# Attention and experts on one core: values and chunk 4's scores as one group, GpSimd scaling chunk 4, and weight pieces begun in output buffers

## The chip, the cores and the metric

The kernel runs on one core of one Trainium2 chip. The metric is device time in microseconds. A core has five engines that run side by side and wait for each other by semaphores: TensorE (PE) multiplies matrices and writes its results to PSUM, a memory of eight banks of 128 x 512 float32 values; VectorE (DVE) and ScalarE (ACT) work on PSUM and on SBUF, the large memory; GpSimd (POOL) works on SBUF; SyncE (SP) issues DMAs. Each engine's instructions stand in an order that is settled when the program is built.

## The reference

Block-causal attention over 8 batches, 8 heads, 576 positions of 64 dimensions (blocks of 64), then a two-layer expert network over all 4608 tokens, with weights given as 64-bit floats:

```python
scores = scale * np.matmul(q, k.transpose(0, 1, 3, 2))
mask = block_i >= block_j
scores = np.where(mask, scores, -1000000000.0)
scores = scores - np.max(scores, axis=-1, keepdims=True)
attn = np.exp(scores)
attn = attn / (np.sum(attn, axis=-1, keepdims=True) + 1e-09)
...
x = np.ascontiguousarray(attn_out.transpose(0, 2, 1, 3)).reshape(B * S, H * D)
h = x @ w_in
g = h * (1.0 / (1.0 + np.exp(-1.702 * h)))
return (g @ w_out).astype(np.float32)
```

## The kernel before

**Turns.** Attention goes by pairs of heads, 32 pairs; turn n (0 to 31) works on pair n, and turn 32 ends the last one. The two heads of a pair lie on partitions 0 to 63 and 64 to 127. Queries are cut into five chunks: chunk 0 has 64 of them, chunks 1 to 4 have 128 each, and chunk i sees 64(2i+1) keys: 64, 192, 320, 448, 576. A score longer than 512 columns does not fit a bank, so chunk 4's is cut into 256 and 320 columns, one bank for each head and cut: four banks.

**Experts.** The 4608 tokens are cut into 12 tiles of 384. A tile has 16 units. A unit is twelve matmuls into the bank `hp` (tag `h`, one buffer), then on ACT a tanh (L562), on DVE the product `g`, which reads `hp` (L563), on ACT the high half `gh` (L571), on GpSimd the low half `gl` (L82); and nine matmuls into the three banks `acc` for the unit before it. Float32 accuracy comes from splitting each operand into a high and a low part.

**Which work stands where.** A string gives each turn's slots (`ORDER`, L26). A number is the scores of that chunk, `3+0/2+1` those of four chunks, `V` the sums of values of the pair before (`av`, L429), `L` the transposes of the next pair's queries and keys (`prep`, L292). `B`, `C` and `a` turn weights by TensorE in the first eight turns; from turn 8 on (`early` false) DVE and 16 DMAs do that (`turn`, L382). After each slot `advance` (L592) emits units of the experts up to a quota, so attention stands between an `hp` block and an `acc` block. The order on DVE, ACT and GpSimd is not written out: the framework's scheduler settles it when it builds the program, with higher priority for `g`, `gh` and `gl`.

**One chunk's way.** Scores lie in banks. `weigh` (L340) reads them on DVE, adds the mask, keeps the maximum (L351, each followed by a short reading of the accumulator), and ACT takes the exponential and the sum (L358). `normalise` (L364) makes the reciprocal on DVE and scales the chunk, on the engine that `SCALE_ON` (L20) names: P for GpSimd, D for DVE. `turn` transposes the result on DVE (L385, L390), and behind chunk 4 issues the 16 DMAs.

**Banks.** `bank()` (L89) hands out PSUM banks in rotation: seven before the experts begin, three while turns 4 to 8 run, four from turn 9 on. The eighth, tag `w3`, belongs until then to the weights: there are 32 pieces of 128 x 512 64-bit words, and `begin` (L215) writes a piece's upper word, scaled, into `w3` by ACT; `merge` (L221) shifts it there on DVE and puts sign and lower bits together in two further instructions; `split_weights` (L239) makes the high and low parts. Output buffers (tag `osb`, three) are idle meanwhile.

Of the kernel before, what the change touches and what calls it, by code (L numbers as in the profile page):

```python
# [16 lines left out]

SCALE_ON = ("PPPPP", "PPPPP", "PPPPD")  # L20

# [4 lines left out]
ORDER = (  # L26
# [3 lines left out]
)  # L30

START = "1+0 - B 2/3 L C - V - 4 - a - - -"
# [8 lines left out]
def attention_moe_kernel(  # L41
# [123 lines left out]
    def width(i):  # L165
        return BLK * (2 * i + 1)
# [47 lines left out]

    def begin(j):  # L215

        bits[j] = ps.tile([P, 512], F32, tag="w3", name="wm")
        for w, c in parts[j]:
            nc.scalar.activation(out=bits[j][:, c], in_=f(w[..., 1]), func=AF.Copy, scale=2.0**-112)

# [71 lines left out]
    def prep(n):  # L292

        tag = "e0" if early(n) and n % 2 else "qk"
        qk[n] = d2.tile([P, 2, S], F32, tag=tag, name="qk", bufs=1)
        for x in range(2):
            nc.vector.transpose(out=qk[n][:, x], in_=raw[n][:, x].rearrange("p c d -> p (c d)"))  # L297
        raw.pop(n)
        m = follower(n)
        if m is not None:  # L300
            load(m)

    stats = {}

    def score(n, banks):

        if n not in stats:
            mx = d2.tile([P, NCH + 1, 2], F32, tag="mx", name="mx")
            sm = d2.tile([P, NCH, 2], F32, tag="sm", name="sm")
            stats[n] = (mx, sm)  # L310
        todo = []
        for chunks in banks:

            part = []
            for lo, hi in ((0, 512),) if width(chunks[0]) <= 512 else ((0, 256), (256, S)):
                ss = [bank() for _ in range(2)]
                c = 0
                for i in chunks:
                    a, z = qrange(i)
                    w = min(hi, width(i)) - lo  # L320
                    for hd in range(2):
                        r = slice(hd * D, hd * D + D)

                        mm(
                            out=ss[hd][:, c : c + w], lhsT=qk[n][r, 0, a : a + P],
                            rhs=qk[n][r, 1, lo : lo + w], start=True, stop=True,
                        )
                        part.append((i, hd, lo, lo + w, ss[hd][0 : z - a, c : c + w]))
                    c += w
            todo.append(sorted(part, key=lambda x: (chunks[::-1].index(x[0]), x[2])))  # L330
        for chunks, part in zip(banks, todo):
            e = {}
            for i, hd, lo, hi, s in part:
                e[i] = weigh(n, i, hd, lo, hi, s, e.get(i))
            for i in chunks[::-1]:
                normalise(n, i, e[i])
                if not early(n):
                    turn(n, i, e[i])
# [87 lines left out]
                in_=src[:, x : x + 2 * len(part), a : a + 2],  # L426
            )

    def av(n):  # L429

        b, h = divmod(n, HP)
        before_av(n)
        o, o0 = bank(), bank()

        todo = []
        for i in range(1, NCH):
            c = (i - 1) * P
            todo += [(o, c, P, j, pw[:, :, SLOT[i] + j]) for j in range(i)]
            todo.append((o, c + BLK, BLK, i, pw[:, 2:4, 9 + i]))
        last = len(todo) - 1  # L440
        todo.append((o0, 0, BLK, 0, pw[:, 0:2, 10]))

        for x, (bk, c, nn, j, w) in enumerate(todo):
            for hd in range(2):
                mm(
                    out=bk[hd * D : hd * D + D, c : c + nn].rearrange("d (a c) -> d a c", c=32),
                    lhsT=values(n)[:, hd, j], rhs=w[:, :, hd], start=x in (0, last + 1), stop=x >= last,
                )
        c0 = (b % 2) * S
        nc.scalar.copy(out=xr[:, h, c0 : c0 + BLK], in_=o0[:, 0:BLK])  # L450
# [5 lines left out]
    def follower(n):  # L456

        m = {0: 2, 1: 3, 2: 4, 3: None}.get(n, n + 1)
        return None if m is None or m >= NPAIR else m

    def order(n):
        return {HP: START, 2 * HP: HANDOVER}.get(n, ORDER[phase(n)]).split()

    def step(n):
# [4 lines left out]
        def item(x):  # L469
            if x == "V":  # L470
                return (lambda: av(n - 1)) if n else None
            if x == "L":
                return (lambda: prep(n + 1)) if n + 1 < NPAIR else None
            if x in ("a", "B", "C"):
# [31 lines left out]
    def chunk_time(tt):  # L506
        return 4 * unit1(tt) + tt // P * 650
# [69 lines left out]
        yield from second(prev)  # L577


    ends = np.cumsum([0.0] + [NFC * chunk_time(tt) for _, tt in TILES])  # L580

    def quota(pos):
        xs, ys = zip(*TILES_BY)
        return -1.0 if pos < xs[0] else np.interp(pos, xs, [ends[y if y >= 0 else y - 1] for y in ys])

    def heads_for(t):
        return -(-sum(TILES[t]) // S) * H
# [36 lines left out]
    for n in range(NPAIR + 1):  # L624
        items = step(n)
        for sl, fn in enumerate(items):
            if fn is not None:
                fn()
            if order(n)[sl] == "V":
# [35 lines left out]
```

## Time and profile before

| | us |
|---|---|
| median of 3 runs | 1122.7 (1121.84 to 1124.51) |
| profiled execution | 1120.49 |
| its span, first to last instruction | 1118.6 |
| PE busy | 1076.4 (96%) |
| DVE, ACT, POOL busy | 583.0, 498.6, 406.7 |
| turn 9 begins at | 218.9 |
| turn 31 begins at | 924.0 |

PE's instructions overlap in its pipeline, so their mean durations do not add up to time; what a block takes is read from the start of its first instruction to the start of the next block's. A turn from the tenth on takes about 32 or 33 us (28 where it holds five units in place of six).

### The profile page before, as it was taken

The page shows a single profiled execution, that of the slowest core. Times are in us where ns is not written, and L with a number is a line of the kernel's source. Part 1 is how long each engine was busy: PE and PEld are TensorE (multiplying, and loading weights), DVE is VectorE, ACT ScalarE, POOL GpSimd, SP SyncE. Part 2 cuts the span into 40 slices and gives each one's busy share as a digit, 9 for nine tenths or more (in the row PEclk, how much of TensorE's full clock was granted, in tenths as well). Part 3 has the DMA queues.
Part 4 walks back from the last instruction along what each step waited for, and adds up shares of the span by engine and source line. Part 5 has one row for each costly group of instructions (what it writes and reads, how often), then busy time and mean ns, then how long its engine had stood idle before and what let it go on. Part 6 is the DMA issues. An engine that isn't in the chain of part 4 may idle for free. (4 is left out here: it accounts for less than half of the span.)

```text
span 1118.6 us, 19977 instructions
## 1 busy us (share of the span) xinstructions
PE 1076.4 (96%) x6960; PEld 908.7 (81%) x6960; DVE 583.0 (52%) x1856; ACT 498.6 (45%) x1321; POOL 406.7 (36%) x509
## 2 busy tenths in 40 slices
PE   5969998999999999999999999999999999999998
PEld 3757776788888888888888888888888888899997
DVE  6776885545545555654555655645545654211210
ACT  5866776434534433534443543444434444322322
POOL 4665664333333332333333333333333233122222
PEclk9979999999999999999999999999999999999999
DMA  8734532332444432343443333344342332200000
GB/s 171 205 89 153 150 73 62 84 79 57 105 86 86 103 80 64 64 98 78 98 101 74 75 93 65 70 108 85 81 107 63 71 85 58 54 29 1 29 1 29
DMA packets 219365, 91.25 MB, mean 82 GB/s; under 512 B 197760, under 2 KB 197760, under 8 KB 219264
## 3 DMA queue, kind: packets, MB, share of 16 engines
q1 hardware_dynamic: 214528, 89.38, 34.0%
q10 hardware_dynamic: 4736, 0.59, 0.3%
q8 instruction: 55, 0.90, 0.3%
q14 instruction: 46, 0.38, 0.1%
HBM read 45.09 MB, written 9.44 MB: 49 GB/s over the span
## 5 line engine op out<-in xcount | busy, mean ns | idle before, releaser
L82 POOL TENSOR_TENSOR gl<-g,gh 128x384 fp32r<-128x384 f32 x192 | 194.7, 1014 | 551.5 <-ACT gh L571 449.1
L99 PE MATMUL hp<-xh,wih 128*128 128x384 f32 x768 | 264.7, 345 | 7.9 <-DVE g L563 6.9
L563 DVE SCALAR_TENSOR_TENSOR g<-g,hp 128x384 f32<-128x384 f32 x192 | 105.9, 552 | 319.1 <-ACT g L562 317.8
L99 PE MATMUL hp<-xh,wil 128*128 128x384 f32 x768 | 258.4, 336 | 0.1
L562 ACT ACTIVATE g<-hp 128x384 f32<-128x384 f32 x192 | 94.1, 490 | 359.8 <-PE hp L99 354.8
L99 PE MATMUL hp<-xl,wih 128*128 128x384 f32 x768 | 253.9, 338 | 0.4 <-DVE xl L82 0.4
L99 PE MATMUL acc<-woh,gh 128*128 128x512 f32 x576 | 233.9, 406 | 0.0
L99 PE MATMUL acc<-wol,gh 128*128 128x512 f32 x576 | 226.9, 394 | 0.0
L99 PEld LDWEIGHTS hp<-xh,wih 128*128 128x128 f32 x768 | 144.2, 188 | 34.1 <-DVE g L563 23.1
L99 PE MATMUL acc<-woh,gl 128*128 128x512 f32 x576 | 167.9, 393 | 0.3 <-POOL gl L82 0.3
L571 ACT CAST gh<-g 128x384 fp32r<-128x384 f32 x192 | 98.4, 513 | 156.5 <-DVE g L563 156.4
L99 PEld LDWEIGHTS hp<-xh,wil 128*128 128x128 f32 x768 | 144.3, 188 | 6.5 <-POOL wil L82 0.7
L358 ACT ACTIVATE e<-e,mx 64x64 f32<-64x64 f32 (+4 forms) x240 | 132.3, 552 | 37.6 <-DVE mx L351 37.6
L376 POOL TENSOR_TENSOR e<-e,sm 64x64 f32<-64x64 f32 (+1 forms) x192 | 113.6, 612 | 95.0 <-DVE sm L371 46.5
L99 PEld LDWEIGHTS hp<-xl,wih 128*128 128x128 f32 x768 | 143.6, 188 | 1.3 <-DVE xl L82 1.3
L99 PE MATMUL bank<-qk 64*128 64x320 f32 (+4 forms) x768 | 122.5, 428 | 14.5 <-DVE qk L297 11.1
L99 PEld LDWEIGHTS acc<-woh,gh 128*128 128x128 f32 x576 | 107.9, 187 | 34.2 <-issue 10.5
L99 PEld LDWEIGHTS acc<-woh,gl 128*128 128x128 f32 x576 | 107.8, 188 | 25.9 <-POOL gl L82 1.2
L99 PEld LDWEIGHTS acc<-wol,gh 128*128 128x128 f32 x576 | 108.3, 188 | 16.7 <-POOL wol L82 0.3
L351 DVE CUSTOM_DVE_ANT_0 e<-bank,mask 64x64 f32<-64x64 f32 (+4 forms) x240 | 89.7, 417 | 56.9 <-PE bank L99 52.8
L385 DVE STREAM_TRANSPOSE turned<-e 128x384 f32<-128x384 f32 (+1 forms) x192 | 92.3, 499 | 48.8 <-POOL e L376 48.3
L99 PEld LDWEIGHTS bank<-qk 64*128 64x128 f32 x768 | 69.6, 193 | 54.2 <-issue 25.4
(50 smaller groups left out, 956.0 us busy)
## 6 DMA issues: line engine op xcount, KB each, us to landing
turned<-turned SPq DMA_DIRECT2D x192, 80.0 KB, 2.1
turned<-turned SPq DMA_DIRECT2D x96, 112.0 KB, 2.2
raw<-in_q_dram SPq DMA_DIRECT2D x128, 72.0 KB, 2.4
out_dram<-osb SPq DMA_DIRECT2D x36, 256.0 KB, 2.2
raw<-in_k_dram SPq DMA_DIRECT2D x120, 72.0 KB, 2.6
turned<-turned SPq DMA_DIRECT2D x96, 88.0 KB, 2.1
words<-in_moe_w_in_dram SPq DMA_DIRECT2D x16, 512.0 KB, 6.3
vp<-in_v_dram SPq DMA_DIRECT2D x60, 128.0 KB, 2.4
```

The lines of the kernel that those rows point to most:

```text
L82: eng.tensor_tensor(out=out, in0=in0, in1=in1, op=ALU.subtract)
L99: return tc.keep_in_program_order(nc.tensor.matmul(**kw))
L351: nc.vector.tensor_tensor_reduce(out=e[0:m, hd, lo:hi], in0=s, in1=mk, op0=ALU.add, op1=ALU.min, scale=-0.125, scalar=3e38 if lo == 0 else ...
L358: nc.scalar.activation(out=e[0:m, hd], in_=e[0:m, hd], func=AF.Exp, scale=-1.0, bias=mx[0:m, i, hd : hd + 1], accum_out=sm[0:m, i, hd : hd ...
L376: nc.gpsimd.tensor_tensor(out=x, in0=x, in1=sc.to_broadcast([m, width(i)]), op=ALU.mult)
L385: nc.vector.transpose(out=tw[:, :, SLOT[i] : SLOT[i] + i, hd].rearrange("p b j c -> p j b c"), in_=e[:, hd, 0 : i * P],)
L562: nc.scalar.activation(out=g, in_=hp[:, 0:tt], func=AF.Tanh, scale=1.702)
L563: nc.vector.scalar_tensor_tensor(out=g, in0=g, scalar=1.0, in1=hp[:, 0:tt], op0=ALU.add, op1=ALU.mult)
L571: nc.scalar.copy(out=gh, in_=g)
```

## The change

- `SCALE_ON`: from turn 8 on chunk 4 is scaled by GpSimd, too.
- A slot `V4` takes the place of `V` and `4` from turn 9 on (turn 8 keeps `HANDOVER`). It takes a bank, runs `av` for the pair before, with the first block of values in that bank's first 64 columns, and then chunk 4's scores. These are now 512 columns for each head in a bank of its own, and the last 64 keys of both heads in one matmul of all 128 rows, in columns 64 to 191 of the bank with the first block of values.
- For that, `prep` leaves the last 64 keys out of `qk` from turn 9's keys on and transposes them into `ends`, where each head's keys have their own columns, with zeros in the other head's rows.
- `av` computes the first block of values ahead of the others, in all turns.
- `begin` writes the first 28 pieces into output buffers in SBUF, and `w3` joins the rotation of banks until these pieces are done.
- The mask grows to 576 columns.

```diff
-SCALE_ON = ("PPPPP", "PPPPP", "PPPPD")
+SCALE_ON = ("PPPPP", "PPPPP", "PPPPP")
...
-    "3+0/2+1 - - - V - - 4 - - - L -",
+    "3+0/2+1 - - - - V4 - - - L - -",
...
         if not turns["experts"]:
             tags += ["acc0", "acc1", "acc2", "h"]
-        elif turns["n"] > 2 * HP:
+        if turns["n"] > 2 * HP or conv["step"] < 4 * len(places):
             tags.append("w3")
...
-    MW = 448
+    MW = 576
...
+    ends = sp.tile([P, 2, BLK], F32, name="ends")
+    nc.gpsimd.memset(ends, 0.0)
...
-        bits[j] = ps.tile([P, 512], F32, tag="w3", name="wm")
+        if j < 2 * len(places):
+            bits[j] = d2.tile([P, WC], F32, tag="osb", name="wb", bufs=3)
+        else:
+            bits[j] = ps.tile([P, WC], F32, tag="w3", name="wb")
...
         for x in range(2):
-            nc.vector.transpose(out=qk[n][:, x], in_=raw[n][:, x].rearrange("p c d -> p (c d)"))
+            z = QC * P if x and n > 2 * HP else S
+            nc.vector.transpose(out=qk[n][:, x, 0:z], in_=raw[n][:, x, 0 : z // 32].rearrange("p c d -> p (c d)"))
+            for hd in range(2 if z < S else 0):
+                r = slice(hd * D, hd * D + D)
+                nc.vector.transpose(
+                    out=ends[r, hd], in_=raw[n][r, x, z // 32 : S // 32].rearrange("p c d -> p (c d)")
+                )
...
-    def score(n, banks):
+    def score(n, banks, shared=None):
...
-            for lo, hi in ((0, 512),) if width(chunks[0]) <= 512 else ((0, 256), (256, S)):
+            cuts = (0, 512) if width(chunks[0]) <= 512 or shared is not None else (0, 256, S)
+            for lo, hi in zip(cuts, cuts[1:]):
...
+            if shared is not None:
+                i = NCH - 1
+                mm(
+                    out=shared, lhsT=qk[n][:, 0, slice(*qrange(i))], rhs=ends.rearrange("p h k -> p (h k)"),
+                    start=True, stop=True,
+                )
+                part += [(i, hd, QC * P, S, shared[:, hd * BLK : (hd + 1) * BLK]) for hd in range(2)]
...
-    def av(n):
+    def av(n, o0=None):
...
-        o, o0 = bank(), bank()
+        o = bank()
+        if o0 is None:
+            o0 = bank()
...
+        todo.insert(0, (o0, 0, BLK, 0, pw[:, 0:2, 10]))
         last = len(todo) - 1
-        todo.append((o0, 0, BLK, 0, pw[:, 0:2, 10]))
...
+    def values_and_4(n):
+        o0 = bank()
+        av(n - 1, o0)
+        if n < NPAIR:
+            score(n, [[NCH - 1]], o0[:, BLK : 3 * BLK])
```

What that moves is shown for turn 18, by the rows of the built programs. `hp_` and `g_` with a number are one unit's, and the two programs number them differently.

PE, before, at the end of the values: `turned` and `vp` are the values' operands, `acc` begins the next unit's work.

```order
L99 MATMUL bank_5492<-turned_75,vp_73 64x128 x6
L99 MATMUL bank_5492<-turned_75,vp_73 64x64 x2
L99 MATMUL bank_5492<-turned_75,vp_73 64x128 x8
L99 MATMUL bank_5492<-turned_75,vp_73 64x64 x2
L99 MATMUL bank_5493<-turned_75,vp_73 64x64 x2
L99 MATMUL acc0_4979<-woh_1335,gh_5457 128x512
```

PE, before, two units further on, where chunk 4's scores (`qk`) stand behind `hp_5568`:

```order
L99 MATMUL hp_5568<-xl_978,wih_1123 128x384
L99 MATMUL bank_5588<-qk_5333 128x256
L99 MATMUL bank_5589<-qk_5333 128x256
L99 MATMUL bank_5592<-qk_5333 128x320
L99 MATMUL bank_5593<-qk_5333 128x320
L99 MATMUL acc0_4979<-woh_1335,gh_5553 128x512
```

PE, after, from the values on: `bank_5516` is the shared bank, and `bank_5554` and `bank_5555` are by the rotation the banks in which chunks 2 and 1 were scored, `bank_5377` and `bank_5378` below.

```order
L99 MATMUL bank_5517<-turned_77,vp_75 64x128 x8
L99 MATMUL bank_5517<-turned_77,vp_75 64x64 x2
L99 MATMUL bank_5554<-qk_5326 128x512
L99 MATMUL bank_5555<-qk_5326 128x512
L99 MATMUL bank_5516<-ends_73,qk_5326 128x128
L99 MATMUL acc0_4973<-woh_1337,gh_5481 128x512
```

The scores of chunk 4 moved ahead by two units, next to the values, and no `acc` or `hp` stands between them any more.

DVE, after, at the same place: `hp_5496` is the last unit ahead of the values.

```order
L595 SCALAR_TENSOR_TENSOR g_5509<-g_5509,hp_5496 128x384
L407 STREAM_TRANSPOSE turned_77<-e_5388 128x3x4x32 x2
L373 ISA e_5405,mx_5369<-bank_5377,mask_69 128x192
L373 ISA mx_5369 128x1
L373 ISA e_5405,mx_5369<-bank_5378,mask_69 128x192
```

The reading of chunks 2 and 1 stands behind that unit's `g` and the two transposes of chunk 3, as it did before.

DVE, before, behind the transposes of chunk 2 (`e_5415`): two units' `g` stand ahead of and within the reading of chunk 4 (`e_5596`).

```order
L385 STREAM_TRANSPOSE turned_75<-e_5415 128x2x4x32 x2
L390 STREAM_TRANSPOSE turned_75<-e_5415 64x2x2x32
L563 SCALAR_TENSOR_TENSOR g_5552<-g_5552,hp_5539 128x384
L351 ISA e_5596,mx_5374<-bank_5588,mask_69 128x256
L351 ISA mx_5374 128x1
L563 SCALAR_TENSOR_TENSOR g_5581<-g_5581,hp_5568 128x384
```

DVE, before, from the end of that reading to the next `g`:

```order
L297 STREAM_TRANSPOSE qk_5655<-raw_5336 128x576 x2
L368 TENSOR_SCALAR sm_5375<-sm_5375 128x2
L371 RECIPROCAL sm_5375<-sm_5375 128x2
L378 TENSOR_SCALAR e_5596<-e_5596,sm_5375 128x576 x2
L385 STREAM_TRANSPOSE turned_75<-e_5596 128x4x4x32 x2
L390 STREAM_TRANSPOSE turned_75<-e_5596 64x2x2x32
L563 SCALAR_TENSOR_TENSOR g_5648<-g_5648,hp_5635 128x384
```

DVE, after, behind the transposes of chunk 2 (`e_5410`):

```order
L407 STREAM_TRANSPOSE turned_77<-e_5410 128x2x4x32 x2
L412 STREAM_TRANSPOSE turned_77<-e_5410 64x2x2x32
L373 ISA e_5559,mx_5369<-bank_5554,mask_69 128x512
L373 ISA mx_5369 128x1
L373 ISA e_5559,mx_5369<-bank_5555,mask_69 128x512
```

DVE, after, from the end of that reading to the first `g` of a unit behind the values, `hp_5598`:

```order
L306 STREAM_TRANSPOSE qk_5647<-raw_5331 128x576
L390 TENSOR_SCALAR sm_5370<-sm_5370 128x2
L393 RECIPROCAL sm_5370<-sm_5370 128x2
L407 STREAM_TRANSPOSE turned_77<-e_5559 128x4x4x32 x2
L412 STREAM_TRANSPOSE turned_77<-e_5559 64x2x2x32
L595 SCALAR_TENSOR_TENSOR g_5611<-g_5611,hp_5598 128x384
```

The whole of chunk 4 now stands directly behind chunk 2, ahead of every `g` of the units behind the values; the two scalings left DVE (GpSimd has them, and the transposes wait for it), and the keys' transposes moved behind that `g`. In other turns of the changed program this `g` stands a few rows further up: between the two 512-wide transposes in turns 12, 13, 14, 17 and 25; right behind the reciprocal in 9, 19, 20, 22, 27, 28 and 30; behind three subtractions for a new tile in 16 and 24. The two transposes of chunk 3 stand ahead of the last unit's `g` in turns 9, 16, 19, 22, 24, 27 and 30, and in turn 10 the whole reading of chunks 2 and 1 does.

More of the change, by code (lines that the diff above doesn't have):

```diff
@@ L446, in av @@
                     out=bk[hd * D : hd * D + D, c : c + nn].rearrange("d (a c) -> d a c", c=32),
-                    lhsT=values(n)[:, hd, j], rhs=w[:, :, hd], start=x in (0, last + 1), stop=x >= last,
+                    lhsT=values(n)[:, hd, j], rhs=w[:, :, hd], start=x in (0, 1), stop=x in (0, last),
                 )
@@ L471, in item @@
                 return (lambda: av(n - 1)) if n else None
+            if x == "V4":
+                return lambda: values_and_4(n)
             if x == "L":
@@ L577, in moe @@
         yield from second(prev)
-    ends = np.cumsum([0.0] + [NFC * chunk_time(tt) for _, tt in TILES])
+    tile_ends = np.cumsum([0.0] + [NFC * chunk_time(tt) for _, tt in TILES])
     def quota(pos):
         xs, ys = zip(*TILES_BY)
-        return -1.0 if pos < xs[0] else np.interp(pos, xs, [ends[y if y >= 0 else y - 1] for y in ys])
+        return -1.0 if pos < xs[0] else np.interp(pos, xs, [tile_ends[y if y >= 0 else y - 1] for y in ys])
     def heads_for(t):
@@ L628, in attention_moe_kernel @@
                 fn()
-            if order(n)[sl] == "V":
+            if order(n)[sl][0] == "V":
                 heads_done = 2 * n
```

## The prediction

> **What bounds the kernel now.** I read the page first, then the windows, then PE's timeline inside one turn, because a share of 96% says that PE is the limit but not where it waits.
>
> ```profile
> span 1118.6 us, 19977 instructions
> PE 1076.4 (96%) x6960; PEld 908.7 (81%) x6960; DVE 583.0 (52%) x1856; ACT 498.6 (45%) x1321; POOL 406.7 (36%) x509
> 0.00:218.90 218.90, 186.05 (x1335) 145.16 (x1335) 155.13 (x472) 143.72 (x394) 122.47 (x152) 0.96 0.48 124
> 252.40:1118.60 866.20, 857.63 (x5413) 735.62 (x5412) 411.10 (x1327) 342.61 (x893) 273.41 (x343) 1.00 0.31 71
> PE hp L99 <- DVE g L563: 6.9, 7, 1.8
> ```
>
> The first nine turns (0 to 218.9 us) hold 32.9 us of idle PE; from the eleventh turn on PE is idle for 8.6 us in 866. So there whatever makes PE wait is added to the time whole. The last row, from PE's waits, names the only engine that can still hold the experts up: VectorE, by reading `hp`. There is one PSUM bank for `hp`, so the next unit's first matmul cannot start until DVE's `g` of the unit before is done.
>
> The middle of a settled turn on PE (the timeline: start and duration in us; each row is the first of its block):
>
> ```profile
> 580.04 2.99 PE L99 MATMUL bank<-turned,vp 128*64 128x128 f32 x60
> 582.96 0.50 PE L99 MATMUL acc<-woh,gh 128*128 128x512 f32 x1
> 585.13 0.33 PE L99 MATMUL hp<-xh,wih 128*128 128x384 f32 x1
> 587.24 0.39 PE L99 MATMUL acc<-woh,gh 128*128 128x512 f32 x1
> 589.37 0.44 PE L99 MATMUL hp<-xh,wih 128*128 128x384 f32 x1
> 591.67 1.24 PE L99 MATMUL bank<-qk 64*128 64x256 f32 x8
> 592.84 0.50 PE L99 MATMUL acc<-woh,gh 128*128 128x512 f32 x1
> ```
>
> The sums of values take 2.92 (580.04 to 582.96), chunk 4's scores 1.17 (591.67 to 592.84), and an `acc` block with an `hp` block behind an attention block 2.17 + 2.11. Two units lie between values and chunk 4. In those 11.6 us DVE does this:
>
> ```profile
> 580.73 0.56 DVE L563 SCALAR_TENSOR_TENSOR g<-g,hp 128x384 f32<-128x384 f32 x1 [3.30 <-ACT g L562]
> 581.21 1.03 DVE L385 STREAM_TRANSPOSE turned<-e 128x384 f32<-128x384 f32 x2
> ...
> 583.35 0.48 DVE L351 CUSTOM_DVE_ANT_0 e<-bank,mask 128x320 f32<-128x320 f32 x1
> 583.76 0.08 DVE L351 DVE_READ_ACCUMULATOR2_ANT mx<- 128x1 f32 x1
> ...
> 588.76 0.55 DVE L563 SCALAR_TENSOR_TENSOR g<-g,hp 128x384 f32<-128x384 f32 x1
> ```
>
> Counted from the start of values: `g` of the unit just before at 0.7; the reading of the scores of chunks 2 and 1 ends at 3.8; their transposes end where the next `g` begins, at 8.7, since DVE stands still for GpSimd's scaling in between. This chain hangs on the last `hp` before the values and keeps its length.
>
> **The merged group, first price: a bank.** Chunk 4's two 512-wide scores take the banks in which chunks 2 and 1 lay. Before, they came two units later and found them empty. Now they follow the values, ready at 2.92, while DVE gives the second bank back at 3.80 (+0.06). The block itself: 1.17 us stood for 256+320 columns a head; 512+128 are 1.3 by the column, less if the fixed part stays; I take 1.25. The group ends at 5.11 after its start, or at 4.17 where nothing is waited for: 0.94 lost. In 15 of the 23 turns DVE's new order has `g` of the last `hp` and both 384-wide transposes ahead of that reading; in seven the transposes stand ahead of that `g`, which frees the bank by their 1.03 earlier and so in time, and in one (the eleventh turn) the reading itself stands ahead. **15 x 0.94 = 14.1 us.**
>
> **Second price: `g` of the first unit behind the group.** PE goes on with `acc` 2.17, `hp` 2.11, `acc` 2.08 (the 2.13 above less its late `g`) and wants the next `hp` at 5.11 + 6.36 = 11.47. DVE reaches that unit's `g` only after all of chunk 4, and chunk 4 only after 8.7. The eleventh turn of before shows how long chunk 4 holds DVE, and that PE does wait for it:
>
> ```profile
> 271.77 0.43 DVE L351 CUSTOM_DVE_ANT_0 e<-bank,mask 128x256 f32<-128x256 f32 x1
> ...
> 272.12 0.55 DVE L563 SCALAR_TENSOR_TENSOR g<-g,hp 128x384 f32<-128x384 f32 x1
> ...
> 273.87 1.44 DVE L297 STREAM_TRANSPOSE qk<-raw 128x576 f32<-128x576 f32 x2
> 275.24 0.17 DVE L368 TENSOR_SCALAR sm<-sm 128x2 f32<-128x2 f32 x1
> 275.44 0.17 DVE L371 RECIPROCAL sm<-sm 128x2 f32<-128x2 f32 x1
> 275.64 0.95 DVE L378 TENSOR_SCALAR e<-e,sm 128x576 f32<-128x576 f32 x2
> 276.51 1.30 DVE L385 STREAM_TRANSPOSE turned<-e 128x512 f32<-128x512 f32 x2
> ...
> 278.17 0.55 DVE L563 SCALAR_TENSOR_TENSOR g<-g,hp 128x384 f32<-128x384 f32 x1
> 278.78 0.45 PE L99 MATMUL hp<-xh,wih 128*128 128x384 f32 x1 [0.85 <-DVE g L563]
> ```
>
> The reading of chunk 4 takes 273.87 - 271.77 = 2.10, less 0.46 for the `g` among it: 1.64 (four instructions over 1152 columns, as 512+512+64+64 are). The sum follows 1.37 later (ACT's two exponentials; two transposes of `qk` fill it, now one), the reciprocal 0.20 after it. So: 8.7, sum at 11.7, reciprocal at 11.9. Then GpSimd in place of DVE's 0.95:
>
> ```profile
> L562 ACT ACTIVATE g<-hp 128x384 f32<-128x384 f32 x192 | 94.1, 490 | 359.8 <-PE hp L99 354.8 <-POOL e L376 4.9
> L376 POOL TENSOR_TENSOR turned<-turned,sm 128x576 f32<-128x576 f32 x16 | 18.0, 1146 | 5.7 <-DVE sm L371 2.6 <-DVE mx L351 2.0 <-ACT xr L450 0.8
> 573.48 0.17 DVE L371 RECIPROCAL sm<-sm 128x2 f32<-128x2 f32 x1
> 573.78 1.82 POOL L376 TENSOR_TENSOR e<-e,sm 128x448 f32<-128x448 f32 x2 [0.54 <-DVE sm L371]
> ```
>
> It starts 0.30 after the reciprocal, at 12.2, and takes 1.15 a head: done at 13.4 and 14.5. DVE transposes the first head beside the second's scaling, the second at 14.6 (half of 1.30), the 64x128 rest (0.36 from there to `g` at 278.17), `g` at 15.6; PE follows 0.61 later: **16.2 instead of 11.45, 4.75 us idle.** Nothing else can fill PE there: its matmuls stand in program order.
>
> Where `g` stands differs by turn: behind all of chunk 4 in nine turns (4.75; 1.9 in the eleventh, whose reading is early), between the two transposes in five (g at 14.1: 3.25), right behind the reciprocal in seven (ACT's tanh, 0.49, is itself behind the exponentials: PE at 12.8; 2.05 in two that have a `qk` transpose between, 1.2 in the five with the early reading), and behind three subtractions of a new tile in two (about 2.8). Sum: 8 x 4.75 + 1.9 + 5 x 3.25 + 2 x 2.05 + 5 x 1.2 + 2 x 2.8 = **72 us.**
>
> **What is saved.** The old late `g` of chunk 4: six turns with 0.85 (such as 278.78) and in each about 0.3 (587.24 to 589.37 is 2.13 for a block that takes 2.08 where nothing is late, the `hp` after it 2.30, of which 0.09 is the step to attention; the turn's other late `g` costs as much): 12 us. One change between attention and experts a turn: values and chunk 4 took 2.92 + 1.17 + 0.18 of switching, now 4.17: 2 us. DVE loses 0.95 of scaling but stands still longer for GpSimd, so that is already in the chain.
>
> **At nothing.** `gl` of that unit stands behind GpSimd's two scalings and needs `gh` (16.8): done at 17.8, wanted by the last third of an `acc` block at 19.8. Chunk 4's 16 DMAs on SP go out at 15.6 and take 2.1 us; the values that read them come a turn later.
>
> ```profile
> L82 POOL TENSOR_TENSOR gl<-g,gh 128x384 fp32r<-128x384 f32 x192 | 194.7, 1014 | 551.5 <-ACT gh L571 449.1 <-issue 62.9 <-PE acc L99 33.2
> turned<-turned SPq DMA_DIRECT2D x192, 80.0 KB, 2.1
> ```
>
> The keys' `ends` (two 64x64 transposes, for 64 columns less) stand behind `g`, and the next turn's scores are due six us later; the bigger mask and the zeros of `ends` fall into the start, before PE's first matmul. The order of the values (first block first) adds no matmul.
>
> **Clock.** PE's granted clock falls after idle stretches:
>
> ```profile
> 56.98:60.39 3.41, 1.35 (x12) 1.04 (x12) 2.91 (x6) 1.15 (x2) 2.55 (x4) 1.00 0.17 28
> 60.39:74.04 13.65, 10.08 (x46) 7.05 (x48) 10.44 (x35) 11.71 (x35) 7.27 (x10) 0.50 0.66 174
> 186.68:190.10 3.42, 1.80 (x14) 1.81 (x15) 0.00 (x0) 1.22 (x4) 1.56 (x2) 1.00 0.00 0
> ```
>
> (Columns: stretch, length, busy time of PE, PEld, DVE, ACT and POOL, granted clock, DMA.) A stretch of 3.41 us in which PE was busy for 1.35 is followed by half clock; one with 1.80 is not, since the 0.96 over the first 218.9 us is 8.8 us lost, 17.5 at half: 13.65 in the second row, the rest at the start. The rows lie on a grid of 3.41 us (four such make 13.65). An idle time of 4.75 leaves some stretch with at most 1.04 busy, one of 3.25 with 1.79 at most and mostly less. Each then costs half of at least one stretch, 1.7; PE is dense behind these waits, so I take one. I count 14 (eight long, five of 3.25, one of the rest): **24 us.** The Trainium skill, "TensorE: Matmul & The Clock Gate", section "What's actually happening", ties the drop to at least one idle window of about 3.4 us; taken as wholly idle, that would spare the waits of 3.25 and three in five of the long ones, and the sum would be 1198. The first row, 40% busy and yet followed by half clock, speaks against so strict a reading.
>
> **The first nine turns.** 28 begun pieces move to SBUF, attention has one bank more.
>
> ```profile
> L223 DVE TENSOR_SCALAR wm<-wm 128x512 uint32<-128x512 uint32 x32 | 22.3, 696 | 15.9 <-ACT wm L219 15.9
> L229 DVE SCALAR_TENSOR_TENSOR wm<-words,wm 128x512 uint32<-128x512 uint32 x28 | 19.3, 688 | 0.3
> L82 DVE TENSOR_TENSOR xl<-xr,xh 128x384 fp32r<-128x384 f32 x48 | 27.1, 605 | 22.5 <-ACT xh L498 22.0 <-PE bank L99 0.5
> ```
>
> DVE's shift takes 696 ns on PSUM; the nearest SBUF row is the scaling above (0.95 for two of 576 columns), so perhaps 0.2 less. Each of its two merges gets an SBUF operand for a PSUM one; the nearest row with two SBUF inputs, 605 ns for 384 columns, says 0.1 more. Net 0; bounds -0.6 and +0.3 a piece, 28 pieces, -17 to +8 us of DVE, of which PE's 32.9 idle can give or take half. I take 0.
>
> **Sum**, against the profiled execution (1120.5; the median of the runs is 2 above it): 1120.5 + 14 + 72 - 14 + 24 = **1217**.
>
> **Rivals.** (1) The clock holds, as after 186.68, or falls only behind wholly idle stretches: 1193 to 1198; chance 0.20. (2) It stays low for more than one stretch (60.39 to 74.04 was four): another 25, 1242; 0.10. (3) Waits half as long, because DVE's chain from values to 8.7 shortens under the new bank order: 1150 to 1175; 0.08. (4) Faster: DVE gets to `g` before PE wants it. It would have to save 4.7 of 15.6 us in the commonest turn; then only the savings remain, with up to 8 in the first nine turns: 1098 to 1107; 0.05. For it speaks only that most of DVE's chain is standing still for GpSimd; against it that all its pieces are measured and its order is fixed. My forecast has 0.57. That the extra bank and the buffers do nothing is inside each of these. The range goes from the first rival less 8 to the second and 4 more (the bounds of the first nine turns): 1185 to 1246. The forecast and these two hold 0.87, and part of the second's tail lies outside. A measurement can tell 0.2% from no change: faster 0.05, the same 0.01, slower 0.94.
>
> **What would show it.** PE's waits: `hp` on DVE `g` should rise from 6.9 to some 70 us, in 23 places of 1.2 to 4.9; a new wait of `bank` on DVE's reading, 0.9 each, in 15 turns; half-clock stretches behind the longest. Turns of 37 us alternating with 33. It is wrong if the turns stay at 32, and its clock term if PEclk is 1.00 throughout.

## The result, and the profile after

The changed kernel takes **1274.24 us** (median of 4 runs, 1272.75 to 1275.31), the kernel before beside it 1122.27 (1120.21 to 1124.51): a ratio of 1.1353, 95% interval 1.1327 to 1.1379. 1217 was forecast, with 1185 to 1246 as its range. The direction was right; 57 us were missing.

The page of the changed kernel, span and busy times:

```profile
span 1273.5 us, 20033 instructions
...
PE 1131.9 (89%) x6914; PEld 955.4 (75%) x6914; DVE 597.2 (47%) x1854; ACT 496.5 (39%) x1321; POOL 467.8 (37%) x558
```

Its windows (columns as in the prediction), cut where turn 9 now begins:

```profile
0.00:263.00 263.00, 208.06 (x1337) 160.54 (x1337) 175.36 (x472) 145.60 (x394) 132.19 (x155) 0.84 0.40 102
263.00:1273.50 1010.50, 923.85 (x5580) 794.83 (x5579) 421.80 (x1382) 350.93 (x927) 335.63 (x403) 0.96 0.28 64
```

PE's two waits from there on (total, times, longest):

```profile
PE hp L99 <- DVE g L595: 75.7, 24, 4.9
PE bank L99 <- DVE mx L373: 7.1, 15, 0.7
```

The kernel before, from its turn 9 on:

```profile
218.90:1118.60 899.70, 890.31 (x5626) 763.50 (x5625) 427.86 (x1384) 354.92 (x927) 284.19 (x357) 1.00 0.31 71
```

Side by side (the first nine turns of before, 218.90 us with PE busy for 186.05, stand in the prediction):

| us | before | after | forecast | measured |
|---|---|---|---|---|
| first nine turns | 218.9 | 263.0 | 0 | +44.1 |
| from turn 9 on, PE idle | 9.4 | 86.7 | +74 | +77.3 |
| from turn 9 on, PE busy | 890.3 | 923.8 | +22 | +33.5 |

(Forecast idle: 14 for the bank, 72 for `g`, less 12 of old waits; forecast busy: 24 of clock less 2 of switching.) The reader should see two separate results. From turn 9 on the forecast of 96 stands beside 110.8. The first nine turns, taken as nothing, lost 44.

What was forecast for the later turns can be read in one of them, turn 18, from the timeline of PE, DVE and POOL after the change:

```profile
607.20 2.99 PE L99 MATMUL bank<-turned,vp 128*64 128x64 f32 x60
607.89 0.55 DVE L595 SCALAR_TENSOR_TENSOR g<-g,hp 128x384 f32<-128x384 f32 x1 [3.63 <-ACT g L594]
...
610.51 0.49 DVE L373 CUSTOM_DVE_ANT_0 e<-bank,mask 128x320 f32<-128x320 f32 x1
...
610.65 1.53 PE L99 MATMUL bank<-qk 64*128 64x512 f32 x4 [0.46 <-DVE mx L373]
...
616.00 0.69 DVE L373 CUSTOM_DVE_ANT_0 e<-bank,mask 128x512 f32<-128x512 f32 x1
...
619.48 0.17 DVE L393 RECIPROCAL sm<-sm 128x2 f32<-128x2 f32 x1
...
619.79 2.25 POOL L398 TENSOR_TENSOR e<-e,sm 128x576 f32<-128x576 f32 x2 [4.73 <-DVE sm L393]
...
622.82 0.31 DVE L412 STREAM_TRANSPOSE turned<-e 64x128 f32<-64x128 f32 x1
...
623.16 0.56 DVE L595 SCALAR_TENSOR_TENSOR g<-g,hp 128x384 f32<-128x384 f32 x1
...
623.77 0.69 PE L99 MATMUL hp<-xh,wih 128*128 128x384 f32 x1 [4.91 <-DVE g L595]
```

Values at 607.20, chunk 4's scores held up by the reading of chunks 2 and 1 until 610.65, the reading of chunk 4 at 616.00, GpSimd's scaling, the transposes, and only then `g` at 623.16: 15.96 after the values' start, where the prediction had 15.6; PE waited 4.91, where it had 4.75.

### The profile page after: what moved, and what is told of

Read it like the earlier page. It is cut to its first block, busy times and chain, and to the rows that moved or that the text cites. A ratio compares the mean times of both kernels' runs of the same rounds, so it can differ in the third digit from the quotient of the medians.

```text
span 1273.5 us, 20033 instructions
## 1 busy us (share of the span) xinstructions
PE 1131.9 (89%) x6914; PEld 955.4 (75%) x6914; DVE 597.2 (47%) x1854; ACT 496.5 (39%) x1321; POOL 467.8 (37%) x558
## 4 chain that ended last, share of the span: by engine, by line
PE 52%; DVE 10%; ACT 6%; POOL 6%; issue 6%; DMA 1%; DVEq 0%; POOLq 0%; SPq 0%; ACTq 0%
PE hp L99 27%; PE acc L99 21%; POOL e L398 6%; ACT e L380 5%; PE bank L99 4%; DVE turned L407 3%; DVE e L373 2%; DVE g L595 1%; DVE turned L412 1%; ACT g L594 1%; DVE sm L390 1%; DVE sm L393 1%; DMA out_dram<-osb 1%; ACT gh L603 0%; DVE mx L373 0%
## 5 line engine op out<-in xcount | busy, mean ns | idle before, releaser
L99 PE MATMUL hp<-xh,wih 128*128 128x384 f32 x768 | 277.2, 361 | 81.2 <-DVE g L595 77.1
L99 PE MATMUL hp<-xh,wil 128*128 128x384 f32 x768 | 271.0, 353 | 0.7 <-POOL wil L82 0.7
L99 PE MATMUL hp<-xl,wih 128*128 128x384 f32 x768 | 266.0, 354 | 0.3 <-DVE xl L82 0.3
L398 POOL TENSOR_TENSOR e<-e,sm 64x64 f32<-64x64 f32 (+4 forms) x240 | 167.7, 720 | 192.2 <-DVE sm L393 149.1
L99 PEld LDWEIGHTS hp<-xh,wih 128*128 128x128 f32 x768 | 153.4, 200 | 105.0 <-DVE g L595 89.7
L99 PE MATMUL bank<-qk 64*128 64x320 f32 (+5 forms) x676 | 131.2, 466 | 35.8 <-DVE mx L373 20.3
L99 PEld LDWEIGHTS hp<-xh,wil 128*128 128x128 f32 x768 | 154.0, 201 | 7.6 <-POOL wil L82 1.1
L99 PEld LDWEIGHTS hp<-xl,wih 128*128 128x128 f32 x768 | 153.1, 200 | 1.0 <-DVE xl L82 1.0
L99 PEld LDWEIGHTS acc<-woh,gh 128*128 128x128 f32 x576 | 113.2, 196 | 24.5 <-ACT gh L603 5.3
L373 DVE CUSTOM_DVE_ANT_0 e<-bank,mask 64x64 f32<-64x64 f32 (+5 forms) x240 | 100.5, 468 | 12.1 <-PE bank L99 6.5
```

The source lines that it names most:

```text
L99: return tc.keep_in_program_order(nc.tensor.matmul(**kw))
L373: nc.vector.tensor_tensor_reduce(out=e[0:m, hd, lo:hi], in0=s, in1=mk, op0=ALU.add, op1=ALU.min, scale=-0.125, scalar=3e38 if lo == 0 else ...
L398: nc.gpsimd.tensor_tensor(out=x, in0=x, in1=sc.to_broadcast([m, width(i)]), op=ALU.mult)
```

## The experiments

Theory 1, formed from the two traces: the first nine turns lose 44 us because the pieces lie in SBUF, where VectorE and GpSimd exclude each other; the rest is lost by VectorE's order. Rivals: something else of the early half (the extra bank, a freer order); and for the later turns, that the group itself or GpSimd's scaling costs PE time in whatever order.

### One half of the change at a time

**late_only**: the change without its early half (pieces in the PSUM bank, the rule of the banks as before).

```diff
-        if turns["n"] > 2 * HP or conv["step"] < 4 * len(places):
+        elif turns["n"] > 2 * HP:
...
-        if j < 2 * len(places):
-            bits[j] = d2.tile([P, WC], F32, tag="osb", name="wb", bufs=3)
-        else:
-            bits[j] = ps.tile([P, WC], F32, tag="w3", name="wb")
+        bits[j] = ps.tile([P, WC], F32, tag="w3", name="wb")
```

> The late half of the change alone: values and chunk 4 as one group with GpSimd scaling it, and the new order of the values; the 28 pieces begin in the PSUM bank again, and attention has no bank more. Theory 1 (the prediction erred in the first nine turns, which lost 44 us to the pieces in SBUF): turn 9 begins at 219 us as before, the part from turn 9 on stays 1010 us long, 1230 in all, with PE waiting some 77 us for DVE's g. Rival A (the early loss is due to something else in the change, such as the order of the values, first block first): turn 9 begins near 263 and the time stays near 1274. Rival B (part of the late loss hangs on the early half): turn 9 at 219, but under 1215 in all.

Measured: 1242.25 us, ratio 1.1048 (1.1029 to 1.1068). Its windows:

```profile
0.00:232.60 232.60, 197.47 (x1337) 155.32 (x1337) 155.55 (x472) 144.38 (x394) 124.87 (x155) 0.91 0.46 116
232.60:1241.10 1008.50, 919.80 (x5580) 791.81 (x5579) 421.60 (x1382) 350.93 (x927) 335.73 (x403) 0.97 0.28 64
```

The second part is as long as with the whole change (1008.5 against 1010.5), so the late loss does not hang on the early half, and rival B falls. But turn 9 begins at 232.6, not at 219: theory 1 was not the whole story of the first nine turns. For 13.7 us of that loss something else of the change is left, as rival A has it.

**avorder**: the kernel before with the first block of values taken first.

```diff
-        todo.append((o0, 0, BLK, 0, pw[:, 0:2, 10]))
+        todo.insert(0, (o0, 0, BLK, 0, pw[:, 0:2, 10]))
...
-                    lhsT=values(n)[:, hd, j], rhs=w[:, :, hd], start=x in (0, last + 1), stop=x >= last,
+                    lhsT=values(n)[:, hd, j], rhs=w[:, :, hd], start=x in (0, 1), stop=x in (0, last),
```

> The kernel before with one edit: the sums of values take the first block first, in all turns. With the late half alone, turn 9 began at 232.6 and not at 218.9. If this order is the cause (PE's first matmul of the values then waits for a bank that VectorE reads last), turn 9 begins at 228 to 236 and the whole is 1132 to 1140. If the cause lies in GpSimd's scaling in turn 8 or in the zeros written at the start: 1121 to 1126.

Measured: 1132.8 us, ratio 1.0077 (1.0046 to 1.0107). Its window of the first nine turns:

```profile
0.00:231.60 231.60, 195.45 (x1335) 153.60 (x1335) 156.01 (x472) 144.26 (x394) 122.37 (x152) 0.92 0.46 117
```

One row of PE's waits there, in this run and then in the kernel before:

```profile
PE bank L99 <- DVE mx L351: 7.7, 5, 4.3
PE bank L99 <- DVE mx L351: 3.4, 5, 1.5
```

So the order that "adds no matmul" is not free: turn 9 begins 12.7 later in the profiled run (8 us in the medians). PE's first matmul of the values now asks for another bank. In turn 8 it waits 4.3 us for VectorE's reading of that bank, where the values of the kernel before waited 1.5. In all PE idles 3.3 longer, and it is busy 9.4 longer at a mean clock of 0.92 in place of 0.96.

**buf_only**: the kernel before with the pieces begun in SBUF; **buf_bank**: this and the extra bank.

```diff
-        bits[j] = ps.tile([P, 512], F32, tag="w3", name="wm")
+        if j < 2 * len(places):
+            bits[j] = d2.tile([P, WC], F32, tag="osb", name="wb", bufs=3)
+        else:
+            bits[j] = ps.tile([P, WC], F32, tag="w3", name="wb")
```

```diff
-        elif turns["n"] > 2 * HP:
+        if turns["n"] > 2 * HP or conv["step"] < 4 * len(places):
```

> The kernel before with one edit: the first 28 pieces begin in SBUF buffers (three in rotation); no bank more. Theory 1 (VectorE's instructions on SBUF wait for GpSimd): the last instruction of a merge, 680 ns before, has a mean near 1190, turn 9 begins near 260, 1160 to 1168 in all. Rival C (the loss comes from the extra bank, which lets attention run ahead and bunches the work): turn 9 within 5 us of 219, 1118 to 1127 in all.

> The kernel before with the early half of the change: pieces begun in SBUF buffers, and the bank that this frees in attention's rotation. Theory 1: as with the buffers alone, to within 5 us (1160 to 1170), turn 9 near 262. Rival C (the bank): this one is 30 us or more slower than the buffers alone. If the bank helps as meant, it is some 5 to 15 us faster than the buffers alone.

Measured: 1159.52 us (ratio 1.0313, 1.0295 to 1.0331) and 1158.54 (1.0306, 1.0286 to 1.0326). The bank changes nothing that can be measured; the buffers alone cost 36. With the buffers alone the time lies a little below its forecast, and so does the mean of the last merge. With the buffers alone, VectorE's two merges among the costliest groups (count, busy time, mean of one), and the last merge of the kernel before, on PSUM:

```profile
L237 DVE SCALAR_TENSOR_TENSOR wm<-words,wb 128x512 uint32<-128x512 uint32 x28 | 29.1, 1041 | 0.6
L232 DVE SCALAR_TENSOR_TENSOR wb<-words,wb 128x512 uint32<-128x512 uint32 x28 | 26.7, 955 | 0.4
L234 DVE SCALAR_TENSOR_TENSOR wm<-words,wm 128x512 uint32<-128x512 uint32 x28 | 19.0, 680 | 0.7
```

And the window of the first nine turns, with PE's longest row of waits in it:

```profile
0.00:258.10 258.10, 203.75 (x1335) 157.59 (x1335) 177.32 (x472) 144.72 (x394) 131.80 (x152) 0.87 0.41 105
PE bank L99 <- DVE mx L354: 13.5, 7, 6.9
```

1041 and 955 ns stand against 680 and 688 on PSUM. VectorE is busy for 22.2 us more (177.32 against 155.13), PE idle for 21.5 more and busy for 17.7 more at the lower clock; its waits for VectorE's reading of the scores are 13.5 in place of 3.4. Why the merges take longer is in the timeline of VectorE and GpSimd:

```profile
70.27 0.69 DVE L232 SCALAR_TENSOR_TENSOR wb<-words,wb 128x512 uint32<-128x512 uint32 x1
...
70.62 1.46 POOL L82 TENSOR_TENSOR wol<-wm,woh 128x512 fp32r<-128x512 f32 x1 [2.54 <-ACT woh L246]
...
71.06 1.57 DVE L237 SCALAR_TENSOR_TENSOR wm<-words,wb 128x512 uint32<-128x512 uint32 x1
```

GpSimd's instruction ends at 72.08. The merge that begins within it, at 71.06, ends at 72.63, 0.55 after that. GpSimd's own, which began within the merge at 70.27, takes 1.46 where it takes 1.28 alone. This is a lock, not a slowdown in proportion: of the 56 merges of this run 23 begin within an instruction of GpSimd, and 22 of them end 545 to 551 ns after that instruction's end, whatever was left of it. The twenty-third began 0.1 us before that end and took 691 ns; the other 33 take 673 to 693. In the kernel before 35 of the 56 begin within one of GpSimd's, and none takes more than 697: there one of the two inputs lies in PSUM.

The lock is seen instruction by instruction. That it accounts for all of the 36 us is argued: VectorE's two merges and its shift are busy for 18.6 us more in this run, ACT's writing of a piece takes 667 ns in place of 634, and no run has the pieces in SBUF without GpSimd at work beside them.

**buf1**: as buf_only, with one buffer in use at a time, so that nothing can run ahead.

```diff
-            bits[j] = d2.tile([P, WC], F32, tag="osb", name="wb", bufs=3)
+            bits[j] = [d2.tile([P, WC], F32, tag="osb", name="wb", bufs=3) for _ in range(3)][0]
```

> The buffers alone, but each piece skips two of the three buffers, so that only one is in use at a time, as with the PSUM bank before. Theory 1 (VectorE waits for GpSimd's instruction whenever both of its inputs lie in SBUF): the merges stay as slow, near 1000 ns in the mean over both, and the whole 1145 to 1165. Rival E (it is the freer order with three buffers, in which pieces run ahead of the attention): the whole 1120 to 1132.

Measured: 1159.69 us (1.0315, 1.0292 to 1.0338), the last merge again 1041 ns in the mean. Rival E falls: the freer order is not the cause.

### GpSimd's scaling

**scale_p**: the kernel before with one entry changed. **late_d**: late_only with that entry as before, so the group with VectorE's scaling.

```diff
-SCALE_ON = ("PPPPP", "PPPPP", "PPPPD")
+SCALE_ON = ("PPPPP", "PPPPP", "PPPPP")
```

> The kernel before with one edit: GpSimd scales chunk 4 from turn 8 on, in place of VectorE. The g behind chunk 4 then waits for two scalings of 1.15 in place of 0.95 on VectorE, some 1.4 later, in most turns: 25 us and, with 2.2 us at most for a wait, little half clock: 1140 to 1160. Rival (VectorE is relieved, and the scheduler puts g first): 1112 to 1122.

> The late half alone, but VectorE scales chunk 4 as before. If GpSimd's scaling is a part of what makes g late (0.30 and 1.15 a head against 0.95 for both, some 1.4 in each turn), PE's waits for g fall from 78 to 40 to 55 us, some half clock goes, and the whole is 1195 to 1225, against 1242 for the late half. If the place of g alone counts: 1235 to 1245.

Measured: 1146.47 us (1.0212, 1.0184 to 1.024) for scale_p: from turn 9 on PE waits for `g` in 23 places, with the clock at 1.00 there.

```profile
PE hp L99 <- DVE g L563: 26.6, 23, 1.8
```

In the kernel before that was 5.1 us in 6 places, so the added waits are 21.5 where 25 were estimated. The run late_d took 1222.26 us (1.0874, 1.0854 to 1.0893), with 62.1 us of waits for `g` against 78.5 in late_only: the whole lies within its forecast, but the waits fell less than forecast. The scheduler found another order there, too: in twelve turns `g` stands between VectorE's scalings of chunk 4 or right behind them, where in late_only it stood behind the reciprocal or between the transposes. So this run does not show the price of GpSimd's scaling by itself.

### VectorE's order

**late_defer**: late_only, with chunk 4's work behind its exponentials put later and held there (`N`: reciprocal and scaling; `T`: transposes).

```diff
-    "3+0/2+1 - - - - V4 - - - L - -",
+    "3+0/2+1 - - - - V4 - - L N - T",
...
+            if chunks == [NCH - 1] and turns["n"] > 2 * HP:
+                kept[n] = e[NCH - 1]
+                continue
...
+        if x == "N":
+            normalise(n, i, kept[n], tc.keep_in_program_order)
+        else:
+            turn(n, i, kept.pop(n), tc.keep_in_program_order)
```

> The late half alone, but the normalising and scaling of chunk 4 stand two slots behind its scores and its transposes two more, and these and the next pair's transposes keep their place on VectorE behind the g of the units traced ahead of them. Nothing else of the group changes: same matmuls in the same order on PE, same banks. Theory 1 (the late loss is the place of g on VectorE): PE's waits for g fall from 77 us to under 10, half clock goes from that part, what stays is the wait for a bank (0.94 in up to 23 turns, 22 us) less the switch saved, so 1115 to 1140 in all. Rival D (the group itself, with 1.3 us more of matmuls in one place, or GpSimd's scaling, delays the units): over 1180.

Measured: 1209.49 us (1.0752, 1.0728 to 1.0777), a miss. Waits from turn 9 on:

```profile
PE hp L99 <- DVE g L607: 35.6, 25, 3.3
PE bank L99 <- DVE mx L376: 16.0, 18, 1.1
PE bank L99 <- DMA turned<-turned: 7.3, 6, 1.9
```

The waits for `g` halved, but they did not go: the reading of chunks 2, 1 and 4 still stood ahead of that `g`. And a new wait came up, for the DMAs that turn the attention weights. By its time this run speaks for rival D (over 1180), which the next runs had to settle.

**defer**: the same deferral on the kernel before, without the group.

```diff
-SCALE_ON = ("PPPPP", "PPPPP", "PPPPD")
+SCALE_ON = ("PPPPP", "PPPPP", "PPPPP")
...
-    "3+0/2+1 - - - V - - 4 - - - L -",
+    "3+0/2+1 - - - V - - 4 L N - T",
```

> The kernel before, without the group and without the early half, but with GpSimd scaling chunk 4, and the normalising and the transposes of chunk 4 each put a unit later, behind that unit's g on VectorE. Theory 1 (what the kernel before still loses from turn 9 on is g behind chunk 4, 0.85 in six turns and 0.3 in each): 1110 to 1117, against 1122. Rival: if those losses come back as waits at the next turn's scores, 1119 to 1126.

Measured: 1238.28 us (1.1012, 1.0986 to 1.1038), 115 more than before where 5 to 12 less was expected. Its timeline, SP's DMAs and PE's next values:

```profile
799.94 1.30 DVE L390 STREAM_TRANSPOSE turned<-e 128x512 f32<-128x512 f32 x2
...
801.27 10.06 SPq L402 DMA_DIRECT2D turned<-turned  x16
...
813.31 4.63 PE L99 MATMUL bank<-turned,vp 128*64 128x128 f32 x60 [4.29 <-DMA turned<-turned]
```

Each DMA lands 2.1 us after its issue, but SP takes 10.06 us to issue the sixteen (seen from its first issue to the end of its last). From the transposes to the values are 13.4 us, and the deferral left less: PE waited 77.1 us in 17 turns for them, and the values ran slower behind each gap (4.63 here for 2.99 at full clock).

**late_written**: late_only with the whole order on VectorE written out from turn 9 on. `keep` holds each of its instructions behind the one traced before; a slot now stands for a portion of work between two `g`: `R` turns chunks 0 and 3 and reads 1 and 2, `W` turns 1 and 2 and reads 4, `LN` prepares the next pair and normalises 4, and the transposes of 4 open the next turn.

```diff
-    "3+0/2+1 - - - - V4 - - - L - -",
+    "3+0/2+1 - - - R - V4 - W - LN -",
...
+    def keep(x):
+        return tc.keep_in_program_order(x) if turns["n"] > 2 * HP else x
```

**written2**: the old order of the values in the first nine turns, and the group one slot later (`Q` normalises 1 and 2). **written3**: chunk 4 is normalised with its reading and turned in its own turn, and the next pair's loads are issued behind the sixteen DMAs.

```diff
-    "3+0/2+1 - - - R - V4 - W - LN -",
+    "3+0/2+1 - - - R - Q V4 W - LN -",
```

```diff
-    "3+0/2+1 - - - R - Q V4 W - LN -",
+    "3+0/2+1 - - - R - Q V4 WN - LT -",
...
+            turn(n, NCH - 1, kept.pop("e4"))
+            if n + 1 < NPAIR and follower(n + 1) is not None:
+                load(follower(n + 1), tc.keep_in_program_order)
```

> The late half alone (group, GpSimd's scaling, order of the values), with VectorE's order from turn 9 on written out: each turn's scores, scalings and transposes are cut into portions, and one portion of 1.6 to 3.7 us stands behind each unit's g. PE has the same matmuls with the group one slot later. Theory 1 (the late loss is only the place of g and of the reading of chunks 2 and 1 on VectorE): waits for g and for banks are both gone from turn 9 on, the clock stays at 1.00 there, that part takes 888 to 900 us as against 1008 with the scheduler's order, and the whole 1115 to 1135. Rival D (the group of 4.2 us on PE, or GpSimd's longer work, delays units in any order): that part stays over 960, the whole over 1190.

> The written-out order of the earlier run with two edits: the values and chunk 4 stand one slot later, so that the 16 DMAs behind chunk 4's transposes (10.06 us for SP to issue, in the run with the deferred transposes, and 2.1 to land) are done before the values want them; and in the first nine turns the first block of values stands last again, as in the kernel before. If the 29 us of waits for those DMAs were what was left of the late loss, the part from turn 9 on takes 888 to 905 us, turn 9 begins at 217 to 222, and the whole is 1108 to 1126. If the group on PE costs something by itself, that part stays over 920 and the whole over 1140.

> As the run before (late half, VectorE's order written out, old order of the values in the first nine turns), but the transposes of chunk 4 stand one unit earlier, in the turn that they belong to, and the next pair's loads behind them on SP. In the run before VectorE's transposes of chunk 3 waited 75 us in 20 turns for the 16 DMAs of the turn before, which read the buffer that they write, and the next g stood behind them. If that was what was left: waits for g fall from 44 us to under 12, the part from turn 9 on takes 888 to 905 us as against 955, and the whole 1108 to 1128. If the group costs PE something by itself: the part stays over 925, the whole over 1148.

Measured: 1175.58 us (1.0462, 1.0434 to 1.0489), 1179.08 (1.0488, 1.0461 to 1.0515) and **1122.79 (0.9992, 0.9983 to 1.0001)**. The first two missed: the part from turn 9 on took 941.7 and 955.4 us, each with a wait for the same DMAs. In late_written `g` was waited for 5.3 us from turn 9 on, and the values waited for the DMAs:

```profile
PE bank L104 <- DMA turned<-turned: 29.3, 11, 7.9
PE hp L104 <- DVE g L639: 5.3, 5, 1.6
```

In written2 the values hardly waited for them (4.1 us), but VectorE did: the transposes of the next chunk 3 write the buffer that the DMAs read. That is a row of VectorE's waits, and `g` stood behind it (PE: 42.4 us).

```profile
DVE turned L428 <- DMA turned<-turned: 75.1, 20, 5.4
```

In written3 PE no longer waits for these DMAs, and VectorE 7.5 us in place of 75.1. Its window from turn 9 on:

```profile
221.60:1121.80 900.20, 886.43 (x5580) 765.63 (x5579) 422.42 (x1382) 351.50 (x927) 336.17 (x403) 1.00 0.31 71
```

PE's waits there:

```profile
PE hp L104 <- DVE g L640: 9.0, 8, 2.9
PE bank L104 <- DVE qk L308: 0.9, 1, 0.9
```

And PE's attention blocks in one turn of its timeline, with the first of the next turn:

```profile
640.06 2.11 PE L104 MATMUL bank<-qk 64*128 64x448 f32 x16
...
659.01 2.98 PE L104 MATMUL bank<-turned,vp 128*64 128x64 f32 x60
...
661.92 1.13 PE L104 MATMUL bank<-qk 64*128 64x512 f32 x4
...
662.98 0.49 PE L104 MATMUL bank<-ends,qk 128*128 128x128 f32 x2
...
671.79 0.65 PE L104 MATMUL bank<-qk 64*128 64x448 f32 x2
```

With the same group of values and chunk 4 and the same scaling on GpSimd, the part from turn 9 on takes 900.2 us where late_only's took 1008.5, the clock is at 1.00, and the whole equals the kernel before within what can be measured. So rival D falls: neither the group nor GpSimd's scaling costs PE this time in every order, and the late loss is VectorE's order and what follows from it. Two other things differ from late_only. The group stands one slot later, as it did in written2, which kept 42.4 us of waits for `g`; and the next pair's loads follow the sixteen DMAs on SP. No run separates those loads from the new place of chunk 4's transposes. A settled turn takes 31.73 (640.06 to 671.79) against 32.19 before (569.47 to 601.66 there); eight remaining waits for `g`, and turn 9 beginning 2.7 later, use that up. No version here beats the kernel before by a measurable amount.

## Why the prediction was wrong

**The step that failed** is the one on the first nine turns: "the nearest row with two SBUF inputs, 605 ns for 384 columns, says 0.1 more", from which followed "Net 0", and bounds of -17 to +8 us. Measured: +44.1 with the whole change. The buffers alone move turn 9 by 39.2, the order of the values alone by 12.7; together they give 44.1 and so do not add up, and no run shows why. Three things were wrong in the step.

- The row was read by its mean. Here are the same 48 instructions of the kernel before, by minimum, median and maximum in ns:

```profile
L82 DVE TENSOR_TENSOR xl<-xr,xh x48: 543/557/1284, 76.2 to 1043.8; 128x384 fp32r<-128x384 f32 x48
```

  A median of 557 and a maximum of 1284 for one form is no spread of a calculation. The long ones, eight above 640, are those that begin within an instruction of GpSimd: the lock was in the trace of before, in the row that was quoted. The Trainium skill states it, on the page "SBUF — State Buffer", section "SBUF: two separate sides": VectorE with two SBUF inputs and GpSimd exclude each other for a whole instruction, and the first to start goes first. The trace agrees, with the 22 merges above that end 545 to 551 ns after GpSimd's instruction.

- The merges cost far more than the 0.1 us each that was added for them. After the change, in the first nine turns, minimum, median and maximum of the last merge:

```profile
L242 DVE SCALAR_TENSOR_TENSOR wm<-words,wb x28: 674/1342/1777, 20.0 to 202.4; 128x512 uint32<-128x512 uint32 x28
```

  That is a mean of 1191 in place of 680, with 841 and 632 for the other two in place of 688 and 696: 16.6 us of VectorE over the pieces, where the bounds ended at +8. The shift did get shorter where GpSimd was idle (near 410 ns), as assumed, but it waits for GpSimd as well (up to 1.5 us), although it has one input only.

- "PE's 32.9 idle can give or take half" priced no clock. PE's idle time rose by 22.0 us (32.9 to 54.9), and its busy time by as much (186.1 to 208.1), with the mean clock down from 0.96 to 0.84.

**The bank, 15 x 0.94 = 14: right.** In 15 turns the values take 3.45 and chunk 4's scores 1.71 (from 610.65 in the timeline above), in the others 2.92 and 1.30: 0.94 apart. The profile books the 0.41 by which the scores take longer as busy PE, so the row of waits says 7.1 and not 14.

**`g` behind chunk 4, 72: right.** 75.7 us in 24 places from turn 9 on, the longest 4.9 for 4.75, and eight turns have a wait of that size, as counted; where 3.25, 2.05 and 1.2 were forecast, most came as 3.3, 2.05 and 1.3. Whole turns run from 31 to 41 us, where 37 and 33 in turn were expected. written3 shows the cause by taking it away.

**Saved, 14:** not shown by itself in the changed kernel. In written3, where little covers it, a settled turn gains 0.46; had every one of the 23 turns gained that, it would be 11.

**Clock, 24: right in kind, too small.** From turn 9 on PE is busy for 33.5 us more; less the 6 of the bank's wait booked there, and with the 2 saved, some 29. 15 stretches ran at half clock where 14 were counted, but seven of them lasted two steps of the grid. One of each, with the stretch ahead of it:

```profile
618.43:621.84 3.41, 0.43 (x2) 0.00 (x0) 1.05 (x3) 1.18 (x4) 2.05 (x2) 1.00 0.01 2
621.84:628.66 6.82, 4.89 (x15) 4.70 (x16) 2.62 (x7) 1.00 (x2) 1.21 (x2) 0.50 0.38 89
580.88:584.29 3.41, 0.31 (x2) 0.00 (x0) 1.32 (x4) 1.08 (x3) 2.16 (x2) 1.00 0.00 0
584.29:587.70 3.41, 3.19 (x10) 3.19 (x11) 1.38 (x4) 0.51 (x1) 1.10 (x2) 0.50 0.26 61
```

The wait that ended at 623.77 lay across a step of the grid: of the next 3.41 us, too, PE was busy for 1.48 only, and half clock went on for another step. "PE is dense behind these waits" holds only for a wait that ends with its stretch. None of the stretches with 0.31, 0.43 and 1.48 was wholly idle, and half clock followed each.

**At nothing:** "Chunk 4's 16 DMAs on SP go out at 15.6 and take 2.1 us" left out the 10.06 that SP needs to issue them. In the changed kernel PE has no wait for them from turn 9 on; in defer (77.1 us of PE's waits), late_written (29.3) and written2 (75.1 of VectorE's) they were the main loss there. And "The order of the values (first block first) adds no matmul" left out the bank that its first matmul now asks for: 12.7 us in avorder.

Of the rivals none came true; of the second, half clock for more than one stretch, a part did, in seven of 15 places. The range could not hold the time, since its upper end took the first nine turns at +4.

## What to carry to other kernels

Before an operand is moved from PSUM to SBUF, ask whether VectorE's instruction then has two SBUF inputs, and what GpSimd does beside it; look at minimum, median and maximum of such rows, not at the mean. A group that saves TensorE two microseconds of switching can cost it a hundred (110.8 here) where one buffer is released by an engine whose order the scheduler decides: write that order out before judging the group. And a transfer's time is that of its issue too: sixteen DMAs behind each other on one queue were a dependence of 12 us here.

## What the runs showed of the hardware

- A merge on VectorE with two SBUF inputs (680 ns alone) that begins within an instruction of GpSimd ends 545 to 551 ns after it (22 of 23 in buf_only): most of its work is held back, not spread out. With one input in PSUM it is not held at all (35 cases in the kernel before, none over 697 ns).
- The shift of 512 columns takes about 410 ns on SBUF when nothing is in the way, and 696 on PSUM. The move was a gain there, but for the waits: the mean after the change is 632, and 731 in buf_only.
- In the changed kernel half clock follows stretches of 3.41 us with PE busy for 0.31, 0.43 or 1.48, and lasts 3.41 or 6.83 by where the wait ends on the grid (eight and seven times from turn 9 on).
- SP issues sixteen DMAs (half of them of 80 KB, the others of 88 and 112) in 10.06 us in defer, 0.63 each, while each lands 2.1 us after its issue (2.2 for 112 KB).
